# Splitting the query maxima on GpSimd instead of VectorE, and one step between them and the query features

## The chip, the cores and the metric

The kernel runs on one core of a Trainium2 chip. The metric is the device time of one execution, in microseconds: before the change the median of three runs is 328.67 us (328.09 to 328.81). The core's engines work side by side, each on its own instruction queue, in order: TensorE (PE in the profile, its weight loads PEld), VectorE (DVE), ScalarE (ACT), GpSimd (POOL) and SyncE (SP), which here only issues transfers. GpSimd's queue issues transfers too.

## The reference, cut to what matters

```
def phi(x):                                   # x: q or k, (8, 8, 576, 64)
    proj = einsum('bhsd,df->bhsf', x, w_phi)  # 128 features
    proj = proj - max(abs(proj), axis=-1)
    return concatenate([exp(proj), exp(-proj)], axis=-1)
q_p, k_p = phi(q), phi(k)
kv  = einsum('bhsf,bhsd->bhfd', k_p, v);  z = sum(k_p, axis=2)
num = einsum('bhsf,bhfd->bhsd', q_p, kv)
den = einsum('bhsf,bhf->bhs', q_p, z)[..., None] + 1e-06
x   = num / den                               # heads joined: (8, 576, 512)

h = maximum(x @ w_in, 0);  u, v = two halves of h, 512 wide each
v_n = layer norm of v;  v_s = einsum('ts,bsd->btd', w_spatial, v_n) + b_spatial
out = (u * v_s) @ w_out                       # (8, 576, 512)
```

The maximum of the absolute projections belongs to a token and a head. The change concerns the maxima of the queries alone.

## The kernel before, in words

**Stage A** (attention) works on 36 units. Each batch gives four pair units (two heads by 512 tokens), and each two batches one tail unit, which holds their last 64 tokens for all heads. In the order of the work unit 0 is a pair, unit 1 the tail of the first two batches, and later each tail unit (9, 18, 27) leads its two batches.

**Stage B** (the gated MLP of a batch) is a list of tasks that is queued when the last x of a batch has been transposed. Each step of the main loop calls `fill(0.25)` four times, which takes tasks off that list by a fixed credit, so stage B's matmuls stand between those of stage A.

Step i of the main loop (L535) writes the work of several units. Call u the unit i, w the unit i-1, z i-2, y i-3, x i-4. In this order:

- `a_keys(u)`, `a_scale(u)`: project the keys (PE L212), their maxima `mk` (DVE L224), the exponentials `kf` (ACT L227), `em` = exp of the key maxima (ACT L239), and on GpSimd v times `em`, `vs` (POOL L244 two times, L246; for a tail unit `vst`, L254 and L256)
- fill; `a_kv(z)` (PE L308, L310, then ACT L312)
- `a_queries(u)`: project the queries (PE L212) and take their maxima `mq` (DVE L233). `a_split(u)`: write them as two bf16 numbers, `mhl` = the rounded maximum (DVE L262) and what rounding left (DVE L263)
- fill; `a_transpose(i+1)` (PE L203, ACT L206 `kT`, DVE L207 `qT`); `a_max_t(w)`: transpose `mhl` of unit w on PE (L267) and copy the 16 rows to `mT` (DVE L268)
- fill; `a_x_t(x)` (PE L336, DVE L337)
- `a_qfeat(w)`: project the queries again with features on the partitions, `pq` (PE L278), subtract the maximum by a matmul of the constant `sel` with `mT` (PE L282; L287 and L289 in a tail unit), and take the exponentials `qf` (ACT L295)
- fill; `a_num(y)` (PE L327) and its division (DVE L317, L318)

So unit w's `mT` is made and used within one step, with one fill and `a_x_t` between. `mhl` and `mT` each lie in three buffers, which the units take in turn; in the listings below they are called mhl_120, mhl_124, mhl_128 and mT_122, mT_126, mT_130. The eight banks of PSUM are handed out in turn to every matmul group.

GpSimd's queue also holds the loads of q and k (L93, L94; tails L80), and stage B's layer norm: four small instructions on 128x4 or less (`root`, L381 to L384) and then `normalize` (L388), four of 128x512 for a batch.

A scheduler moves instructions a little against the order in which the code writes them, on each engine. At the start the spatial weights are loaded (`wsp`, `wspt`) and transposed after step 4 (L175, L177).

Of the kernel before, what the change touches and what calls it, by code (L numbers as in the profile page):

```python
# [9 lines left out]
BF16 = mybir.dt.bfloat16  # L10
AF = mybir.ActivationFunctionType
ALU = mybir.AluOpType
# [4 lines left out]
def kernel(  # L17
# [15 lines left out]
    nc = tc.nc  # L33

    B, H, S, D = q.shape
# [4 lines left out]
    P = 128  # L40
# [11 lines left out]
    a1 = ctx.enter_context(tc.tile_pool(name="stage_a", bufs=2))  # L52
# [93 lines left out]


    NM = 3
    mhl, mT = [], []
    for i in range(NM):  # L150
        t = cpool.tile([P, P], BF16, name=f"mhl{i}")
# [42 lines left out]
    def a_transpose(u):  # L194
        src = st[u["b"]] if u["pair"] else gs[u["g"]]
        pt = psum.tile([P, 2, 4, P], BF16, tag="bank", name="pt")
        for i, x in enumerate((src["k"], src["q"])):
            for j in range(4):
                if u["pair"]:
                    blk = x[:, 2 * u["pj"] + j // 2, (j % 2) * P:(j % 2 + 1) * P]  # L200
                else:
                    blk = x[:, 2 * j:2 * j + 2, :]
                nc.tensor.transpose(out=pt[:, i, j, :], in_=blk, identity=ident)  # L203
        u["kT"] = a1.tile([P, 4, P], BF16, tag="kT", name="kT")
        u["qT"] = a1.tile([P, 4, P], BF16, tag="qT", name="qT", bufs=3)
        nc.scalar.copy(out=u["kT"], in_=pt[:, 0])  # L206
        nc.vector.tensor_copy(out=u["qT"], in_=pt[:, 1])  # L207

# [7 lines left out]
    def a_keys(u):  # L216

        u["mk"] = small.tile([P, H], FP32, tag="mk", name="mk")
        u["kf"] = feat.tile([P, 2, H, F], BF16, tag="kf" if u["pair"] else "kf_t", name="kf",
                            bufs=4 if u["pair"] else 2)  # L220
        for half in range(2):
            pk = by_token(u["kT"], half)
            hs = slice(4 * half, 4 * half + 4)
            nc.vector.tensor_reduce(out=u["mk"][:, hs], in_=pk, axis=AX.X, op=ALU.max,  # L224
                                    apply_absolute_value=True)
            for s, sc in ((0, 1.0), (1, -1.0)):
                nc.scalar.activation(out=u["kf"][:, s, hs, :], in_=pk, func=AF.Exp, bias=0.0, scale=sc)  # L227

    def a_queries(u):
        u["mq"] = small.tile([P, H], FP32, tag="mq", name="mq")  # L230
        for half in range(2):
            pq = by_token(u["qT"], half)
            nc.vector.tensor_reduce(out=u["mq"][:, 4 * half:4 * half + 4], in_=pq, axis=AX.X, op=ALU.max,  # L233
                                    apply_absolute_value=True)

    def a_scale(u):
        em = small.tile([P, 2, H], FP32, tag="em", name="em")
        for s, sc in ((0, -1.0), (1, 1.0)):
            nc.scalar.activation(out=em[:, s, :], in_=u["mk"], func=AF.Exp, bias=0.0, scale=sc)  # L239
        if u["pair"]:  # L240
            pj = u["pj"]
            vs = feat.tile([P, 2, H, DA], BF16, tag="vs", name="vs", bufs=4)
            for s in range(2):
                nc.gpsimd.tensor_tensor(out=vs[:, s, :, 0:D], in0=st[u["b"]]["v"][:, pj * H:(pj + 1) * H, :],  # L244
                                        in1=em[:, s, :].unsqueeze(2).to_broadcast([P, H, D]), op=ALU.mult)
            nc.gpsimd.tensor_copy(out=vs[:, :, :, D:DA], in_=em.unsqueeze(3).to_broadcast([P, 2, H, 2]))  # L246
            u["vs"] = vs
        else:
            d = gs[u["g"]]
            vs = vst[u["g"] % 2]  # L250
            for bl in range(2):
                r = slice(bl * TL, (bl + 1) * TL)
                for s in range(2):
                    nc.gpsimd.tensor_tensor(out=vs[r, bl, s, :, 0:D], in0=d["v"][r],  # L254
                                            in1=em[r, s, :].unsqueeze(2).to_broadcast([TL, H, D]), op=ALU.mult)
                nc.gpsimd.tensor_copy(out=vs[r, bl, :, :, D:D + 1].rearrange("p i n o -> p i (n o)"), in_=em[r])  # L256
            d["vs"] = vs
            d["unit"] = u

    def a_split(u):  # L260
        m = mhl[u["i"] % NM]
        nc.vector.tensor_copy(out=m[:, 0:H], in_=u["mq"])  # L262
        nc.vector.tensor_tensor(out=m[:, H:2 * H], in0=u["mq"], in1=m[:, 0:H], op=ALU.subtract)  # L263

    def a_max_t(u):
        pt = psum.tile([P, P], BF16, tag="bank", name="pt")
        nc.tensor.transpose(out=pt, in_=mhl[u["i"] % NM], identity=ident)  # L267
        nc.vector.tensor_copy(out=mT[u["i"] % NM][0:2 * H, :], in_=pt[0:2 * H, :])  # L268

    def a_qfeat(u):  # L270

        m = mT[u["i"] % NM]
        u["qf"] = []
        for half in range(2):
            pq = psum.tile([P, 4, P], FP32, tag="bank", name="pq")
            if u["pair"]:
                for par in range(2):
                    nc.tensor.matmul(out=pq[:, 2 * par:2 * par + 2, :], lhsT=wphi2[:, par * F:(par + 1) * F],  # L278
                                     rhs=u["qT"][:, 2 * half:2 * half + 2, :], start=True, stop=False)
                    for x in range(2):  # L280
                        j = 4 * half + 2 * x + par
                        nc.tensor.matmul(out=pq[:, 2 * par + x, :], lhsT=sel[:, j, :], rhs=m,  # L282
                                         start=False, stop=(x == 1))
            else:
                for x in range(4):
                    h = 4 * half + x
                    nc.tensor.matmul(out=pq[:, x, :], lhsT=wphi2[:, (h % 2) * F:(h % 2 + 1) * F],  # L287
                                     rhs=u["qT"][:, h // 2, :], start=True, stop=False)
                    nc.tensor.matmul(out=pq[:, x, :], lhsT=sel[:, h, :], rhs=m, start=False, stop=True)  # L289
            if u["pair"]:  # L290
                qf = feat.tile([P, 2, 4, P], BF16, tag="qf", name="qf", bufs=7)
            else:
                qf = feat.tile([P, 2, 4, P], BF16, tag="qf_t", name="qf_t", bufs=4)
            for s, sc in ((0, 1.0), (1, -1.0)):
                nc.scalar.activation(out=qf[:, s], in_=pq, func=AF.Exp, bias=0.0, scale=sc)  # L295
            u["qf"].append(qf)
# [199 lines left out]
    def unit(i):  # L496
        return units[i] if 0 <= i < NU else None
# [30 lines left out]
    def fill(share):  # L528
        credit[0] = min(credit[0] + RATE * share, RATE / 2)
        while queue and credit[0] >= queue[0][0] / 2:  # L530
            cost, task = queue.pop(0)
            task()
            credit[0] -= cost

    def step(i):  # L535
        n, u, w, z, y, x = (unit(i + d) for d in (1, 0, -1, -2, -3, -4))
        if i == 0:
            a_transpose(u)
        if u:
            a_keys(u)  # L540
            a_scale(u)
        fill(0.25)
        if z and z["pair"]:
            a_kv(z)
        if u:
            a_queries(u)
            a_split(u)
        fill(0.25)
        if n:
            a_transpose(n)  # L550
        if w:
            a_max_t(w)
        fill(0.25)
        if x and x["pair"]:
            a_x_t(x)
            if x["pj"] == NP - 1:
                g, bl = x["g"], x["b"] % 2
                alone = g in SPLIT
                if alone or bl == 1:
                    tail_x_t(g, [bl] if alone else [0, 1])  # L560
                queue.extend(b_tasks(x["b"]))
        if w:
            a_qfeat(w)
        fill(0.25)
        if y and y["pair"]:
            a_num(y)
            if y["pj"] == NP - 1:
                g, bl = y["g"], y["b"] % 2
                alone = g in SPLIT
                if alone or bl == 1:  # L570
                    tail_num(g, [bl] if alone else [0, 1])

    def on_pair(i):
        u = unit(i)
        return u if u and u["pair"] else None

    for i in range(NU + 4):
        u = unit(i)
# [47 lines left out]
```

## Time and profile before

| what | before |
| --- | --- |
| median of three runs | 328.67 us (328.09 to 328.81) |
| the profiled execution | 327.9 us, of which span 326.1 us |
| TensorE busy | 284.8 us, 87% of the span |
| VectorE busy | 244.3 us, 75% |
| ScalarE busy | 242.3 us, 74% |
| GpSimd busy | 173.8 us, 53% |
| the two instructions of the split (L262, L263) | 36 each, 14.6 and 17.8 us of VectorE |

The span runs from the first to the last instruction; 1.8 us of the profiled execution lie around it. Times within the trace are microseconds from the start of the span. A row of a timeline gives the start, how long it lasted, the engine and line, and in brackets how long the engine had been idle ahead of it and what ended that. Rows with xN put N instructions of one line together. Matmuls overlap in PE's pipeline and their ends are modelled, so a PE that shows busy may still have short gaps in it.

### The profile page before, as it was taken

The numbers are of one execution on the slowest core, as the hardware profiler recorded it, in microseconds if no ns is written. First come the engines' busy times: TensorE is split into PE (matmuls) and PEld (weight loads), VectorE is DVE, ScalarE is ACT, GpSimd is POOL, SyncE is SP. The second block draws the span as 40 slices with busy tenths as digits, with TensorE's granted clock in tenths as the row PEclk, the third lists the DMA queues.
The fourth block names the chain that finished last, engine by engine and source line by source line (L and its number), as shares of the span: only waits on it lengthen the run. The fifth ranks groups of instructions, "written<-read, shape, count | busy, mean of one in ns | idle before, by whom it ended". The sixth has DMA issues, their size and how long they took to land.

```text
span 326.1 us, 8471 instructions
## 1 busy us (share of the span) xinstructions
PE 284.8 (87%) x3327; PEld 196.4 (60%) x3370; DVE 244.3 (75%) x626; ACT 242.3 (74%) x546; POOL 173.8 (53%) x263
## 2 busy tenths in 40 slices
PE   0485888899999899989899999999799999979884
PEld 0274677566666577657667677766577676534431
DVE  7685799698987989798798997598788983622430
ACT  3488598889498888798899668998898647433603
POOL 8299827678254756548586362527655220250520
PEclk9999899999999999999999999999999999999979
DMA  7999997931079009940732088410000004302104
GB/s 102 225 159 253 194 238 76 133 107 35 2 130 271 6 0 131 250 92 1 100 74 90 0 106 239 169 43 2 0 2 2 1 2 181 114 0 102 46 0 145
DMA packets 43773, 31.17 MB, mean 96 GB/s; under 512 B 14355, under 2 KB 38099, under 8 KB 43733
## 3 DMA queue, kind: packets, MB, share of 16 engines
q0 software_dynamic: 27856, 13.77, 31.2%
q1 hardware_dynamic: 15876, 16.85, 16.9%
q8 instruction: 26, 0.43, 0.5%
q14 instruction: 15, 0.11, 0.1%
HBM read 32.85 MB, written 9.44 MB: 130 GB/s over the span
## 4 chain that ended last, share of the span: by engine, by line
PE 39%; DVE 32%; DMA 11%; ACT 10%; POOL 4%; issue 2%; SPq 1%; POOLq 0%; ACTq 0%; DVEq 0%
PE po L468 8%; DVE mq L233 6%; PE ps L445 6%; DVE stats L374 6%; DVE mk L224 5%; DMA wspt<-in_moe_w_spatial_dram 5%; DMA out_dram<-ob 4%; PE ps L212 3%; PE pq L282 3%; ACT qf L295 3%; ACT kf L227 3%; DVE x L318 3%; PE pn L327 3%; PE pu L424 2%; PE pv L308 2%
## 5 line engine op out<-in xcount | busy, mean ns | idle before, releaser
L244 POOL TENSOR_TENSOR vs<-v_f,em 128x512 bf16<-128x512 f32 x64 | 65.5, 1044 | 56.1 <-ACT em L239 46.8
L227 ACT ACTIVATE kf<-ps 128x512 bf16<-128x512 f32 x144 | 77.4, 631 | 11.7 <-DVE mk L224 11.6
L295 ACT ACTIVATE qf<-pq 128x512 bf16<-128x512 f32 x128 | 67.1, 639 | 15.6 <-PE pq L282 15.3
L224 DVE TENSOR_REDUCE mk<-ps 128x4 f32<-128x512 f32 x72 | 47.2, 674 | 1.2 <-PE ps L212 1.1
L233 DVE TENSOR_REDUCE mq<-ps 128x4 f32<-128x512 f32 x72 | 46.4, 679 | 2.1 <-PE ps L212 2.1
L470 ACT COPY ob<-po 128x512 f32<-128x512 f32 (+1 forms) x38 | 23.2, 609 | 27.3 <-issue 17.5
L445 PE MATMUL ps<-w_spT,vn 128*128 128x512 bf16 x115 | 34.0, 392 | 5.2 <-POOL vn L388 4.5
L448 DVE TENSOR_TENSOR uT<-ps,uT 128x512 bf16<-128x512 f32 x32 | 21.9, 683 | 17.7 <-PE ps L446 17.7
L282 PE MATMUL pq<-mT,sel 128*128 128x128 bf16 x256 | 28.8, 221 | 6.8 <-DVE mT L268 6.8
L374 DVE BATCH_NORM_STATS2 stats<-vr 128x6 f32<-128x512 bf16 (+1 forms) x38 | 25.6, 681 | 12.1 <-ACT vr L373 11.8
L278 PE MATMUL pq<-qT,wphi 128*128 128x256 bf16 x128 | 31.2, 277 | 2.4 <-ACT kf L227 1.8
L424 PE MATMUL pu<-xT,w_in_bf 128*128 128x512 bf16 x120 | 31.6, 379 | 1.4 <-ACT vr L373 0.7
L371 PE MATMUL pv<-w_in_bf,xT 128*128 128x512 bf16 x118 | 31.7, 379 | 1.1 <-ACT kf L227 0.4
L468 PE MATMUL po<-w_out_bf,uT 128*128 128x512 bf16 x118 | 31.0, 379 | 0.5
L282 PEld LDWEIGHTS <-sel 128*128 128x128 bf16 x256 | 23.8, 99 | 12.5 <-issue 10.3
L206 ACT COPY kT<-pt 128x512 bf16<-128x512 bf16 x36 | 22.6, 628 | 8.4 <-PE pt L203 6.6
L373 ACT ACTIVATE vr<-pv 128x512 bf16<-128x512 f32 (+1 forms) x38 | 24.0, 639 | 6.5 <-PE pv L371 5.8
L308 PEld LDWEIGHTS <-kf 128*128 128x128 bf16 x512 | 23.7, 99 | 6.0 <-ACT qf L295 0.7
L318 DVE TENSOR_TENSOR x<-pn,rc 128x256 bf16<-128x256 f32 x64 | 26.2, 419 | 0.9
L327 PEld LDWEIGHTS <-qf 128*128 128x128 bf16 x512 | 20.5, 98 | 9.4 <-issue 4.7
L327 PE MATMUL pn<-kv,qf 128*128 128x66 bf16 x512 | 22.4, 194 | 3.6 <-ACT kv L312 2.3
L212 PE MATMUL ps<-wphi,kT 128*128 128x256 bf16 x144 | 23.3, 286 | 2.3 <-ACT kT L206 2.3
(111 smaller groups left out, 622.6 us busy)
## 6 DMA issues: line engine op xcount, KB each, us to landing
out_dram<-ob SPq DMA_DIRECT2D x32, 256.0 KB, 2.4
v_f<-in_v_dram SPq DMA_DIRECT2D x6, 1024.0 KB, 6.5
k_bf<-in_k_dram POOLq DMA_DIRECT2D x7, 512.0 KB, 6.1
q_bf<-in_q_dram POOLq DMA_DIRECT2D x7, 512.0 KB, 7.7
v_f<-in_v_dram POOLq DMA_DIRECT2D x2, 1024.0 KB, 8.7
v_tl<-in_v_dram SPq DMA_DIRECT2D x8, 128.0 KB, 4.2
w_in_bf<-in_moe_w_in_dram POOLq DMA_DIRECT2D x1, 1024.0 KB, 12.8
out_dram<-ob SPq DMA_DIRECT2D x8, 128.0 KB, 2.4
```

Source lines behind the costliest of these rows:

```text
L224: nc.vector.tensor_reduce(out=u["mk"][:, hs], in_=pk, axis=AX.X, op=ALU.max, apply_absolute_value=True)
L227: nc.scalar.activation(out=u["kf"][:, s, hs, :], in_=pk, func=AF.Exp, bias=0.0, scale=sc)
L233: nc.vector.tensor_reduce(out=u["mq"][:, 4 * half:4 * half + 4], in_=pq, axis=AX.X, op=ALU.max, apply_absolute_value=True)
L244: nc.gpsimd.tensor_tensor(out=vs[:, s, :, 0:D], in0=st[u["b"]]["v"][:, pj * H:(pj + 1) * H, :], in1=em[:, s, :].unsqueeze(2).to_broadcast( ...
L282: nc.tensor.matmul(out=pq[:, 2 * par + x, :], lhsT=sel[:, j, :], rhs=m, start=False, stop=(x == 1))
L295: nc.scalar.activation(out=qf[:, s], in_=pq, func=AF.Exp, bias=0.0, scale=sc)
L318: nc.vector.tensor_tensor(out=x, in0=pn[r, :, 0:D], in1=rc[r].to_broadcast([n, 4, D]), op=ALU.mult)
L327: nc.tensor.matmul(out=pn[:, pos, :], lhsT=u["qf"][hh][:, s, pos, :], rhs=d["kv"][:, 2 * u["pj"] + hh, s, :], start=(s == 0), stop=(s == 1))
L374: nc.vector.bn_stats(out=stats[r], in_=dst[r])
L424: nc.tensor.matmul(out=pu, lhsT=w_in_bf[:, kc, dc * P:(dc + 1) * P], rhs=d["xT"][:, kc, :], start=(kc == 0), stop=(kc == KC - 1))
L445: nc.tensor.matmul(out=ps, lhsT=d["vn"][:, sp, cs], rhs=w_spT[:, sp, 0:T0], start=(sp == 0), stop=False)
L468: nc.tensor.matmul(out=po[r], lhsT=lhs(dc), rhs=w_out_bf[:, dc, :], start=(dc == 0), stop=(dc == KC - 1))
```

## The change

The split is issued on GpSimd, other than for the first seven units (0 to 6), which keep it on VectorE. `a_qfeat` is called for unit z instead of w, that is one step later than `a_max_t` of the same unit. `qT`, which then lives a step longer, gets five buffers instead of three. The unused function `on_pair` goes.

```diff
+    EARLY = 7
...
-        u["qT"] = a1.tile([P, 4, P], BF16, tag="qT", name="qT", bufs=3)
+        u["qT"] = a1.tile([P, 4, P], BF16, tag="qT", name="qT", bufs=5)
...
     def a_split(u):
         m = mhl[u["i"] % NM]
-        nc.vector.tensor_copy(out=m[:, 0:H], in_=u["mq"])
-        nc.vector.tensor_tensor(out=m[:, H:2 * H], in0=u["mq"], in1=m[:, 0:H], op=ALU.subtract)
+        eng = nc.vector if u["i"] < EARLY else nc.gpsimd
+        eng.tensor_copy(out=m[:, 0:H], in_=u["mq"])
+        eng.tensor_tensor(out=m[:, H:2 * H], in0=u["mq"], in1=m[:, 0:H], op=ALU.subtract)
...
-        if w:
-            a_qfeat(w)
+        if z:
+            a_qfeat(z)
         fill(0.25)
```

Three places show what this does to the queues. In the changed kernel the line numbers are one higher up to the split and two higher behind it.

VectorE, where unit 8 is split (buffer mhl_128) and unit 7's transposed maxima are copied (mT_126). Before:

```order
L233 TENSOR_REDUCE mq<-ps 128x4 x2
L207 COPY qT<-pt 128x512
L262 CAST mhl_128<-mq 128x8
L268 COPY mT_126<-pt 16x128
L263 TENSOR_TENSOR mhl_128<-mq,mhl_128 128x8
L337 COPY xT<-pt 128x512
```

and now:

```order
L234 TENSOR_REDUCE mq<-ps 128x4 x2
L208 COPY qT<-pt 128x512
L270 COPY mT_126<-pt 16x128
L339 COPY xT<-pt 128x512
L367 COPY xTt<-pt 128x4x64
```

The two instructions of the split are gone from VectorE's queue, here and for every unit from 7 on, 58 in all.

GpSimd at the same stage, from the tail unit 9 (its last instruction is the CAST to vst_138) to unit 10, with the layer norm of the first batch between. Before:

```order
L256 CAST vst_138<-em 64x16
L381 TENSOR_SCALAR var<-mv 128x4
L382 TENSOR_TENSOR rs<-var,neghalf 128x4
L383 TENSOR_TENSOR var<-mv,rs 128x4
L384 TENSOR_SCALAR rs<-var 128x4
L388 TENSOR_SCALAR vn<-vr,rs 128x512 x4
L244 TENSOR_TENSOR vs<-v_f,em 128x8x64 x2
L246 CAST vs<-em 128x16x2
```

and now:

```order
L257 CAST vst_138<-em 64x16
L264 CAST mhl_120<-mq 128x8
L265 TENSOR_TENSOR mhl_120<-mq,mhl_120 128x8
L383 TENSOR_SCALAR var<-mv 128x4
L384 TENSOR_TENSOR rs<-var,neghalf 128x4
L385 TENSOR_TENSOR var<-mv,rs 128x4
L386 TENSOR_SCALAR rs<-var 128x4
L390 TENSOR_SCALAR vn<-vr,rs 128x512 x4
L245 TENSOR_TENSOR vs<-v_f,em 128x8x64 x2
L247 CAST vs<-em 128x16x2
L264 CAST mhl_124<-mq 128x8
L265 TENSOR_TENSOR mhl_124<-mq,mhl_124 128x8
```

The split stands behind the unit's product with v, and behind whatever layer norm was queued ahead of that. The transfers that GpSimd issues keep their order; they now have the split between them.

TensorE at the first places where the query features follow the transpose of the maxima with nothing between, the transpose being that of buffer mhl_124 (unit 1). Before:

```order
L267 LDWEIGHTS mhl_124
L267 MATMUL pt<-ident,mhl_124 128x128
L287 LDWEIGHTS wphi_76
L287 MATMUL pq<-qT,wphi_76 128x128
L287 LDWEIGHTS wphi_76
L287 MATMUL pq<-qT,wphi_76 128x128
L289 LDWEIGHTS sel
L289 MATMUL pq<-mT_126,sel 128x128
```

and now:

```order
L269 LDWEIGHTS mhl_124
L269 MATMUL pt<-ident,mhl_124 128x128
L280 LDWEIGHTS wphi_76
L280 MATMUL pq<-qT,wphi_76 128x256
L284 LDWEIGHTS sel
L284 MATMUL pq<-mT_122,sel 128x128
```

The matmuls with `sel` read the `mT` of the unit before (mT_122, unit 0) instead of the one whose transpose has just been issued (mT_126, unit 1). At the start this also means that the features of unit 2, not those of unit 3, are the last ahead of the transposes of the spatial weights. At the end the features of the last two units stand one step later among stage B's last matmuls of batch 6.

More of the change, by code (lines that the diff above doesn't have):

```diff
@@ L571, in step @@
                     tail_num(g, [bl] if alone else [0, 1])
-    def on_pair(i):
-        u = unit(i)
-        return u if u and u["pair"] else None
     for i in range(NU + 4):
```

## The prediction

> **What bounds the kernel now.** I read the page's busy line and chain first, then a table of stages, then PE's waits in the long middle stage.
>
> ```profile
> PE 284.8 (87%) x3327; PEld 196.4 (60%) x3370; DVE 244.3 (75%) x626; ACT 242.3 (74%) x546; POOL 173.8 (53%) x263
> PE 39%; DVE 32%; DMA 11%; ACT 10%; POOL 4%; issue 2%; SPq 1%; POOLq 0%; ACTq 0%; DVEq 0%
> ```
>
> PE is busiest and holds most of the chain of waits, but DVE holds a third of it. No engine bounds the whole, so the stage matters. The split of units 7 to 35, which moves, lies between 52 and 270 us:
>
> ```profile
> core 0: us, PE busy (x) PEld busy (x) DVE busy (x) ACT busy (x) POOL busy (x), PEclk, DMA share, GB/s
> 52.00:270.00 218.00, 204.60 (x2581) 147.04 (x2616) 185.12 (x472) 183.41 (x424) 123.73 (x184) 1.00 0.39 76
> 270.00:326.00 56.00, 47.06 (x349) 23.20 (x353) 19.89 (x50) 23.45 (x42) 13.53 (x26) 0.96 0.25 85
> ```
>
> There PE works 94% of the time, DVE 85%, ACT 84%. PE is in order and stands still 218.00 - 204.60 = 13.4 us. Whatever takes those stops away shortens the stage. The waits of PE between 52 and 270 us say what they are (line, releaser, us in total, times, longest):
>
> ```profile
> PE pq L282 <- DVE mT L268: 6.3, 11, 1.2
> PE pq L278 <- ACT kf L227: 1.6, 3, 0.7
> PE pq L289 <- DVE mT L268: 1.4, 2, 1.1
> ...
> PE pn L327 <- DVE mq L233: 0.3, 1, 0.3
> ```
>
> 6.3 + 1.4 = 7.7 us, more than half, is one wait: the matmul with `sel` waits for DVE's copy of the transposed maxima. One such place, around the tail unit 18:
>
> ```profile
> 143.06 0.22 PE L267 MATMUL pt<-ident,mhl 128*128 128x128 bf16 x1
> ...
> 144.56 2.04 POOL L244 TENSOR_TENSOR vs<-v_f,em 128x512 bf16<-128x512 f32 x2 [4.42 <-issue]
> ...
> 145.65 0.98 DVE L262 CAST mhl<-mq 128x8 bf16<-128x8 f32 x1
> ...
> 147.04 0.18 DVE L268 COPY mT<-pt 16x128 bf16<-16x128 bf16 x1
> ...
> 147.27 0.22 PE L289 MATMUL pq<-mT,sel 128*128 128x128 bf16 x1 [1.13 <-DVE mT L268]
> ```
>
> The transpose ended at 143.28, but its copy came at 147.04, behind DVE's queue, with the next unit's split in it. The cast of 8 numbers per partition took 0.98 us there and ended at 146.63, just as GpSimd's two products did (144.56 + 2.04 = 146.60). The split's cost on DVE is mostly such waiting:
>
> ```profile
> L262 DVE CAST mhl<-mq x36: 157/334/1128, 15.0 to 262.5; 128x8 bf16<-128x8 f32 x36
> L263 DVE TENSOR_TENSOR mhl<-mq,mhl x36: 122/481/1085, 15.2 to 262.9; 128x8 bf16<-128x8 f32 x36
> 52.00:270.00 218.00, 12.62 (x29) 1.00 0.39 76
> 52.00:270.00 218.00, 15.01 (x29) 1.00 0.39 76
> ```
>
> The last two rows are these lines' busy time in the stage: 12.62 + 15.01 = 27.6 us for 29 units, 0.95 us each, against 157 + 122 ns for the shortest of the two.
>
> **The change part by part.**
>
> *The features one step later.* A unit's `mT` is now copied in one step and first read in the next. A step lasts about 7.5 us (218 us for 29), longer than the 3.8 us from transpose to copy above, so the 7.7 us of stops go. Bounds: 7.7 us if PE meets nothing else late, and nothing if each is replaced. The next things late on PE are in the list above, ACT's `kf` and DVE's `mq`: small, and not tied to this order. I take 7.0 us. The 8.7 - 7.7 = 1.0 us of such waits before 52 us I don't count, since a transfer ends that stage (below).
>
> ```profile
>   DVE mT L268: 8.7, 15
> ```
>
> *27.6 us off DVE.* Nothing is queued on DVE in their place. What that brings beyond the stops is bounded below by nothing (DVE is off the end of the stage) and above by the split's share of the chain of waits, which was largest between 60 and 110 us:
>
> ```profile
> by line: DMA out_dram<-ob 13.4%; DVE mq L233 9.5%; DVE stats L374 8.8%; DVE mk L224 8.5%; ACT qf L295 8.3%; DVE x L318 5.7%; ACT kf L227 5.6%; DVE mhl L262 4.7%; ACT vr L373 4.1%; DVE uT L448 3.8%; DVE mhl L263 3.4%; PE pq L282 3.2%; DVE qT
> ```
>
> There it is 4.7 + 3.4 = 8.1% of 50 us. PE has only 13.4 - 7.7 = 5.7 us of other visible stops to give, so that is the upper end here. I take 0.7 us, near the lower end: those stops name ACT more than DVE.
>
> *58 small instructions on GpSimd.* The trace has no split there. Nearest rows by shape:
>
> ```profile
> L382 POOL TENSOR_TENSOR rs<-var,neghalf 128x4 f32<-128x4 f32 x8 | 8.3, 1043 | 0.7
> L246 POOL CAST vs<-em 128x32 bf16<-128x32 f32 x32 | 6.8, 212 | 6.3 <-ACT em L239 6.3
> L383 POOL TENSOR_TENSOR var<-mv,rs 128x4 f32<-128x4 f32 x8 | 1.6, 205 | 0.6
> ```
>
> and the distance from one dependent instruction to the next:
>
> ```profile
> 223.05 0.20 POOL L383 TENSOR_TENSOR var<-mv,rs 128x4 f32<-128x4 f32 x1
> 223.34 0.25 POOL L384 TENSOR_SCALAR rs<-var 128x4 f32<-128x4 f32 x1
> ```
>
> A cast of 128x32 is 0.21 us, a product of 128x4 0.21 us, start to start 0.29: about 0.6 us a unit, 17 us in all; GpSimd goes to 124 + 17 = 141 of 218 us. From above, both like L382, a power: 2 x 1.04 + 0.2 = 2.3 us a unit. From below, DVE's 0.28. The split is a cast and a plain subtraction, so I take 0.6.
>
> What waits for GpSimd is new: PE's `a_max_t` (L267), and the whole of PE behind it. Queued behind the split on GpSimd are the next `vs`, the layer norm and the loads. The split stands behind the unit's `vs`, so its slack is from the end of L246 to L267 of the same unit. The pairs of units 7, 10, 29 and 30:
>
> ```profile
> 56.45 0.21 POOL L246 CAST vs<-em 128x32 bf16<-128x32 f32 x1
> 57.86 0.22 PE L267 MATMUL pt<-ident,mhl 128*128 128x128 bf16 x1
> ...
> 80.19 0.21 POOL L246 CAST vs<-em 128x32 bf16<-128x32 f32 x1
> 81.44 0.22 PE L267 MATMUL pt<-ident,mhl 128*128 128x128 bf16 x1
> ...
> 217.92 0.21 POOL L246 CAST vs<-em 128x32 bf16<-128x32 f32 x1
> 222.89 0.22 PE L267 MATMUL pt<-ident,mhl 128*128 128x128 bf16 x1
> ...
> 228.74 0.21 POOL L246 CAST vs<-em 128x32 bf16<-128x32 f32 x1
> 230.04 0.22 PE L267 MATMUL pt<-ident,mhl 128*128 128x128 bf16 x1
> ```
>
> They leave 1.2, 1.0, 4.8 and 1.1 us. Five of the 29 units leave under 1.4 us, the first and the last of them being 7 and 30 and their sum 6.0; the others, like 29, leave over 2. With 0.6 us a unit only unit 10 is late: unit 9's split stands in the same unbroken run of GpSimd, so 80.40 + 1.2 = 81.6, late by 0.2. Steps that shorten by some 0.2 us take that from every slack. I take a loss of 0.5 us, between 0 and 5.5 (at 2.3 us a unit the five lose 11.5 - 6.0).
>
> The Trainium skill speaks against the move: GPSIMD Engine Reference, section 4.1 Engine selection, wants elementwise work on VectorE and calls GpSimd about twice as slow for two inputs. Applied to DVE's means here (435 and 518 ns) an estimate by that page is 0.44 + 1.04 = 1.5 us a unit; the five narrow units would lose 7.5 - 6.0 = 1.5 us instead of 0.5, and the sum below would be 323.2. Applied to DVE's shortest it is 0.4 us a unit, which the rows above bear out better.
>
> *The start.* Until 38 us all goes at the pace of a transfer:
>
> ```profile
> 38.12 0.22 PE L177 MATMUL pt<-ident,wspt 64*128 64x64 bf16 x1 [1.06 <-DMA wspt<-in_moe_w_spatial_dram]
> ...
> 39.00 2.06 ACT L295 ACTIVATE qf<-pq 128x512 bf16<-128x512 f32 x4 [1.33 <-PE pq L282]
> ...
> 39.93 0.61 PE L212 MATMUL ps<-wphi,kT 128*128 128x256 bf16 x4
> ...
> 41.48 0.60 ACT L227 ACTIVATE kf<-ps 128x512 bf16<-128x512 f32 x1
> ```
>
> Units 0 to 6 stay on DVE, and that load is issued ahead of any split on GpSimd, so it lands as before. Unit 3's features, which ACT made from 39.00 on, now come a step later, so ACT has nothing until the keys of 39.93 are through: at most 40.5 - 39.0 = 1.5 us of ACT's time lost, at least nothing. I take 0.7.
>
> *The end.* The features of two units move into a stretch where PE is filled with stage B's last tasks; PE has the same sum to do. Cover gone, it would cost the four exponentials of a unit, 2.06 us. I take 0. `qT`'s buffers cost nothing: no transfer and no instruction more.
>
> Sum: -7.0 - 0.7 + 0.5 + 0.7 = -6.5 us. The profiled execution took 327.9 us (326.1 of span and 1.8 around it), so 321.4. The runs' median lies 328.67 - 327.9 = 0.8 above that execution: **322.2 us**.
>
> **The rivals.**
>
> *More than the stops.* If DVE's split paced the stage together with PE, its removal also closes other stops. Most it can give is all of PE's 13.4 us; I price it at 10 to 13: 316 to 319. For it: 8.1% of the chain in one stretch. Against: ACT, at 183.4 of 218 us, is not relieved.
>
> *Another wait takes its place.* PE arrives 0.27 us a step earlier at matmuls that need ACT's `kT` and `kf` or a bank of PSUM, and stands there instead. Then the 7.7 us come back but for a little: 327.5 to 329.3. For it: ACT's 84%. Against: 13 of PE's stops named `mT` and few named ACT.
>
> *GpSimd is late for PE (slower).* One mechanism: PE's L267 waits for the split behind `vs` and the layer norm. It decides against the change when two instructions on GpSimd cost some 2.3 us a unit. The five narrow units then lose 5.5 us, GpSimd goes to 124 + 67 = 191 of 218 us, and its `vs` and layer norm fall behind by 0.5 us in about ten more units: -6.5 - 0.5 + 5.5 + 5 = +3.5, 332.2 us (330 to 335). For it: 1.04 us on L382. Against: L246 and L383.
>
> *The change does not do what it says.* Excluded by the two queues: the split has left DVE's, and L284 reads the earlier `mT`.
>
> **How the numbers follow.** Forecast 0.61 (own range 319.5 to 325.5: the taken value, and its terms moved half way to their bounds), more than the stops 0.14, another wait 0.13, GpSimd late 0.12. Low 317.0 leaves out the far half of the second, high 328.2 the upper part of the third and all of the last. A measurement of this kernel tells 0.2% (0.66 us) from no change, which is 328.0 to 329.3. The third case lies there for 0.09 of its 0.13 and below for 0.04. So faster 0.61 + 0.14 + 0.04 = 0.79, same 0.09, slower 0.12.
>
> **What would show it.** Right, if PE's waits name `mT` for under 1 us, the stage of units 7 to 35 is 6 to 7 us shorter, and the split on GpSimd shows 0.2 to 0.3 us for each instruction. PE waiting for `mhl` on GpSimd for over 2 us would show the term of 0.5 too small; PE waits on ACT grown by 5 us the third case; a DVE gap with no PE stop left, the second. I am wrong if the stage keeps its length although the waits for `mT` are gone.

## The result and the profile after

| what | before | after | forecast |
| --- | --- | --- | --- |
| median, runs side by side on one chip | 328.38 us (327.0 to 328.81) | 319.53 us (318.53 to 319.81) | 322.2 us (317.0 to 328.2) |
| ratio | | 0.973, 95% interval 0.970 to 0.977 | 0.980 |
| the profiled execution, its span | 327.9, 326.1 us | 318.53, 316.8 us | 321.4 us |

Medians and ranges here and below leave out executions that took over 1.5% longer than the fastest of their kernel.

The change makes the kernel faster by 2.7%, by 8.9 us from median to median. In the same unit as the forecast's sum, the profiled execution, it brought 327.9 - 318.5 = 9.4 us where the sum had 6.5. Both profiled executions were faster than their medians, the one before by 0.5 us and the one after by 1.0.

The busy line and the engines' part in the chain of waits, after:

```profile
PE 284.4 (90%) x3370; PEld 196.6 (62%) x3370; DVE 223.7 (71%) x568; ACT 241.0 (76%) x546; POOL 183.5 (58%) x321
PE 66%; DVE 10%; DMA 7%; ACT 7%; POOL 6%; issue 1%; SPq 1%; POOLq 0%; ACTq 0%; DVEq 0%
```

DVE's share of the chain fell from 32% to 10%, and PE, with the same matmuls to do, now holds two thirds of it. Note the matmul count: all 3370 were recorded here, 3327 in the profile of before. So a little of what the trace of before showed as idle PE was PE at work.

To see where the time went, both spans are cut at the same two places of the program: the transposes of the query maxima (`a_max_t`) of units 7 and 35. The stretches are the start, the 28 steps in between, and the end. First before, then after (columns: length, busy time and count of PE, PEld, DVE, ACT, POOL, PE's granted clock, DMA share, GB/s):

```profile
0.00:57.86 57.86, 38.01 (x489) 30.45 (x490) 44.60 (x123) 41.32 (x96) 40.63 (x58) 0.97 1.11 178
57.86:267.44 209.58, 197.22 (x2471) 140.97 (x2505) 178.58 (x452) 176.28 (x407) 119.68 (x179) 1.00 0.38 77
267.44:326.10 58.66, 49.57 (x376) 25.01 (x379) 21.13 (x53) 24.75 (x44) 13.53 (x26) 0.96 0.24 82
```

```profile
0.00:57.02 57.02, 36.59 (x478) 29.81 (x478) 46.20 (x121) 38.78 (x91) 41.09 (x60) 0.94 1.13 180
57.02:256.68 199.66, 196.04 (x2506) 140.76 (x2505) 156.42 (x395) 175.54 (x407) 128.87 (x235) 1.00 0.40 81
256.68:316.80 60.12, 51.74 (x395) 26.00 (x391) 21.12 (x53) 26.71 (x48) 13.56 (x26) 0.96 0.24 80
```

The middle stretch became 209.58 - 199.66 = 9.9 us shorter. Two more profiles of the unaltered changed kernel show it 200.3 and 199.7 us long, so it varies by some 0.6 us. The start became 0.8 us shorter and the end 1.5 us longer, but one unit's features went from the first to the last (PE's 12 weight loads for it: 490 to 478, and 379 to 391; about 1 us of PE's time, by the timeline of another unit, 139.68 to 140.73), so neither place lost or won as much as 1 us beside that. The end varies more than that from profile to profile, and with the clock granted in it: with the same features in it, it took 58.4 us at a clock of 0.99, 59.6 to 60.1 at 0.96 and 61.4 to 61.6 at 0.93. In the middle PE stood idle for 199.66 - 196.04 = 3.6 us, before for 12.4 by the trace. Of these 12.4 an estimated 1.5 to 2 are the 35 matmuls missing there: a second profile of the changed kernel that lacks 37 of them (below) shows 5.7 us idle. So PE's visible stops went from some 10.5 us to 3.6.

What is left of them in the middle stretch of the changed kernel, and the one wait for `mT` in its whole span, which lies in the start (line, releaser, us, times, longest):

```profile
PE pq L280 <- ACT kf L228: 1.9, 2, 1.1
PE pv L373 <- DVE xTt L367: 0.4, 1, 0.4
...
PE ps L447 <- POOL vn L390: 0.3, 1, 0.3
```

```profile
PE pv L310 <- DVE mT L270: 0.6, 1, 0.6
```

No wait for `mT` is left in the middle, and no matmul waits for `mhl`. The same place that the prediction showed, the tail unit 18, now reads:

```profile
138.36 0.22 PE L269 MATMUL pt<-ident,mhl 128*128 128x128 bf16 x1
...
141.37 0.18 DVE L270 COPY mT<-pt 16x128 bf16<-16x128 bf16 x1
...
145.31 0.22 PE L291 MATMUL pq<-mT,sel 128*128 128x128 bf16 x1
```

The copy still comes 2.8 us after the transpose, behind DVE's queue. But nobody needs it before 145.31.

The split itself, by its lines (shortest, median, longest in ns; first and last start), and from the same view how long PE's weight loads sat idle until it was there (us, times):

```profile
L264 POOL CAST mhl<-mq x29: 181/191/205, 56.5 to 253.2; 128x8 bf16<-128x8 f32 x29
L265 POOL TENSOR_TENSOR mhl<-mq,mhl x29: 195/201/217, 56.8 to 253.4; 128x8 bf16<-128x8 f32 x29
L264 DVE CAST mhl<-mq x7: 157/306/1033, 14.6 to 47.9; 128x8 bf16<-128x8 f32 x7
L265 DVE TENSOR_TENSOR mhl<-mq,mhl x7: 135/168/1001, 14.8 to 49.0; 128x8 bf16<-128x8 f32 x7
...
  POOL mhl L265: 0.2, 1
```

On GpSimd it takes 0.19 + 0.20 = 0.39 us, every time. In the seven units that DVE kept, it still reaches 1.0 us for one instruction.

### The profile page after: what moved, and what is told of

The parts are those of the page before. It is cut to its first block, busy times and chain, and to the rows that moved or that the text cites. A ratio compares the mean times of both kernels' runs of the same rounds, so it can differ in the third digit from the quotient of the medians.

```text
span 316.8 us, 8543 instructions
## 1 busy us (share of the span) xinstructions
PE 284.4 (90%) x3370; PEld 196.6 (62%) x3370; DVE 223.7 (71%) x568; ACT 241.0 (76%) x546; POOL 183.5 (58%) x321
## 4 chain that ended last, share of the span: by engine, by line
PE 66%; DVE 10%; DMA 7%; ACT 7%; POOL 6%; issue 1%; SPq 1%; POOLq 0%; ACTq 0%; DVEq 0%
PE po L470 11%; PE ps L447 9%; PE ps L213 8%; PE pv L373 6%; PE pu L426 5%; DMA wspt<-in_moe_w_spatial_dram 5%; PE pv L310 4%; PE pn L329 4%; PE pt L204 4%; PE pq L280 3%; PE pq L284 3%; DVE stats L376 3%; ACT kf L228 3%; POOL vn L390 3%; PE ps L448 2%; DMA bsp_row<-in_moe_b_spatial_dram 2%
## 5 line engine op out<-in xcount | busy, mean ns | idle before, releaser
L447 PE MATMUL ps<-w_spT,vn 128*128 128x512 bf16 x128 | 35.4, 392 | 4.4 <-POOL vn L390 4.4
L280 PE MATMUL pq<-qT,wphi 128*128 128x256 bf16 x128 | 30.3, 274 | 3.2 <-ACT kf L228 2.1
L284 PE MATMUL pq<-mT,sel 128*128 128x128 bf16 x256 | 30.3, 220 | 0.0
L284 PEld LDWEIGHTS <-sel 128*128 128x128 bf16 x256 | 25.1, 98 | 5.7 <-issue 3.6
L208 DVE COPY qT<-pt 128x512 bf16<-128x512 bf16 x36 | 15.1, 420 | 17.2 <-ACT kT L207 17.2
```

The lines of the kernel that those rows point to most:

```text
L447: nc.tensor.matmul(out=ps, lhsT=d["vn"][:, sp, cs], rhs=w_spT[:, sp, 0:T0], start=(sp == 0), stop=False)
```

## The experiments

Two theories stood at the outset. A, the forecast's: the later step takes away PE's stops for `mT`, and that is nearly all; DVE's relief brings little. B: the relief of DVE carries a good part of the gain itself, since DVE's queue is what makes `mT` and other things late.

### The step alone

```diff
-    EARLY = 7
+    EARLY = 99
```

The split of all units stays on DVE; the features come a step later.

> The features one step later, the split left on VectorE for all units. Theory A (the gain is TensorE's stops for the copied maxima): these stops go with the step alone, 7.0 of the stage's us, so 321 to 322.5 us, with under 1 us of TensorE waits that name mT. Theory B (VectorE's 27.6 us of splits pace the stage): VectorE keeps them all, so little comes, 325.5 to 328 us.

Measured: 322.74 us (320.36 to 324.75), ratio to the kernel before 0.982 (0.975 to 0.990). The middle stretch, and PE's waits in it that are over 0.4 us:

```profile
57.45:260.59 203.14, 198.01 (x2507) 141.09 (x2505) 178.91 (x451) 175.38 (x407) 119.34 (x179) 1.00 0.40 79
```

```profile
PE pq L280 <- ACT kf L228: 2.0, 2, 1.2
PE pv L373 <- DVE xTt L367: 0.8, 2, 0.6
```

203.14 against 209.58: the step brings 6.4 us there, and no wait for `mT` is left. DVE works as long as before (178.9 us). The rest of the change, 203.14 - 199.66 = 3.5 us, is then the split's. Theory B's 325.5 to 328 is excluded, and theory A's mechanism is borne out, though the time lies 0.2 us above its range. From median to median of the runs beside it (327.57 us before) the step brought 4.8 us.

### The split alone

```diff
-        if z:
-            a_qfeat(z)
+        if w:
+            a_qfeat(w)
```

The split is on GpSimd from unit 7 on; the features stay in the step of `a_max_t`.

> The split on GpSimd from unit 7 on, the features in the same step as the transpose of the maxima, as before. Theory A: the copy of the maxima stands less deep in VectorE's queue, since 0.95 us a unit is gone from it, but is still read in the same step; about half of the 7.7 us of stops goes, 324 to 326 us, and 3 to 5 us of TensorE waits still name mT. Theory B: nearly all of the gain, 319.5 to 322 us.

Measured: 322.35 us (321.27 to 323.67), ratio 0.982 (0.976 to 0.988). The middle stretch, and the largest of PE's waits in it:

```profile
56.89:260.25 203.36, 197.93 (x2507) 140.88 (x2505) 157.11 (x396) 176.06 (x407) 128.53 (x235) 1.00 0.40 79
```

```profile
PE pq L284 <- DVE mT L270: 2.2, 5, 0.8
```

This is where theory A fails. Without the later step the split's move brings 6.2 us in the middle, almost as much as the step. It does so by the same stops: with the split out of DVE's queue `mT` is copied sooner, and PE's waits for it shrink to 2.2 + 0.2 us (the second at L291). So the two parts are cures for the same stops, and by the waits they overlap: the step alone takes away all 7.7 us, the split's move alone 5.3. In the middle stretch they bring 6.4 and 6.2 us alone and 9.9 together, from one profile of each. The medians can't tell this: 4.8 and 5.2 us alone make 10.0, where both together bring 8.9, and the runs of one kernel spread over more than that difference. Theory B's range (319.5 to 322) is 0.4 us away, within the spread of the runs.

Both kernels have `qT`'s five buffers, so neither shows what these bring by themselves. Before the change DVE's copy into `qT` waited this much, and for nothing else (us, times):

```profile
  ACT kT L206: 10.1, 13
```

It never waited for PE to be done with an old `qT`, so there was no such stop for more buffers to take away.

### All units on GpSimd

```diff
-    EARLY = 7
+    EARLY = 0
```

> The changed kernel with the split on GpSimd for all units, the first seven too. If the first seven stand on VectorE to keep GpSimd's queue free for the transfers of the start: the splits of units 0 and 1 and their waits stand ahead of or between these, wspt lands 0.6 to 2 us later than 38.1, and as much comes on the time, 320 to 321.5 us. Rival: the splits fit between the issues and the landing stays at 38, 319 to 319.8 us.

Measured: 323.16 us (322.27 to 324.57), ratio 0.984 (0.978 to 0.991): the changed kernel loses some 3 us by it, more than the 320 to 321.5 expected. The transpose of unit 7 came at 61.14, not 57.02. PE's waits until there that are not for a transfer, and GpSimd's queue:

```profile
PE pv L312 <- POOL vst L257: 5.0, 1, 5.0
PE pt L269 <- POOL mhl L265: 4.2, 2, 2.7
...
PE pt L269 <- ACT kT L207: 2.5, 1, 2.5
```

```profile
22.36 0.80 POOL L136 DMA_DIRECT2D w_out_bf<-in_moe_w_out_dram  x1
23.16 2.07 POOL L255 TENSOR_TENSOR vst<-v_tl,em 64x512 bf16<-64x512 f32 x2
...
27.80 0.19 POOL L264 CAST mhl<-mq 128x8 bf16<-128x8 f32 x1
...
28.95 0.20 POOL L265 TENSOR_TENSOR mhl<-mq,mhl 128x8 bf16<-128x8 f32 x1
```

In the first 30 us GpSimd issues the transfers of the weights, and unit 1's products stand behind these issues, and its split behind those: it ends at 29.15. Nothing here is late because of the split's own 0.4 us. Nor is it the reason that was expected: the load of `wspt` was issued at 21.83, no later than in the changed kernel (22.3), and PE did not wait for it. So the units that kept the split on DVE did so with cause, but not all seven: with `EARLY = 4`

```diff
-    EARLY = 7
+    EARLY = 4
```

> The changed kernel with the split on GpSimd from the 5th unit on, not the 8th (the first four on VectorE). A try for a faster kernel. Theory (the first units on GpSimd stand behind the issue of transfers there, and cost 4 us at the start when all are): those that are left come after the issues, so the start is within 1 us of the changed kernel's, 319 to 321. Rival (each unit of the first seven on GpSimd costs its share of the 4 us): +1.5 us, 321.5.

it took 319.49 us (318.19 to 320.23), beside 318.68 us (317.93 to 319.94) of the changed kernel on the same chip: nothing won, and nothing lost that these runs can show.

### The last unit's features moved back

```diff
-        if z:
-            a_qfeat(z)
+        if z and i <= NU:
+            a_qfeat(z)
+        if i == NU:
+            a_qfeat(w)
```

> The changed kernel with the features of the last unit moved back to the step of the unit before, so that the end stands as before the change. The prediction's term for the end is 0: 319.5 us within 0.7. Rival: the later features hold up the end by the four exponentials of a unit or part of them, then 317.5 to 318.8 us.

Measured: 320.69 us (318.71 to 321.65), ratio 0.975 (0.967 to 0.983). That is above the 319.5 within 0.7 that was expected, and away from the rival's 317.5 to 318.8. The end took 61.37 us at a clock of 0.93, beside 61.52 at the same clock in the kernel with `EARLY = 4`, whose end is that of the changed kernel. No gain: that the last features come later at the end costs nothing that can be measured.

### VectorE's time put back, without the split

What did the split's move bring beyond the stops for `mT`: DVE's time, or something about the split? Here the changed kernel gets work on DVE that nobody reads, at the split's old place. In the first kernel:

```diff
+        if u["i"] >= EARLY:
+            dum = small.tile([P, 2, 6], FP32, tag="dum", name="dum")
+            x = u["qT"].rearrange("p a b -> p (a b)")
+            nc.vector.bn_stats(out=dum[:, 0, :], in_=x[:, 0:128])
```

> The changed kernel, and for each unit from the 7th on VectorE takes the statistics of 128 columns of qT once more, with nothing reading the result: some 0.28 us a unit (an estimate from the shortest records of the two split instructions on VectorE, 0.148 + 0.122 us), 8 us in all, put back on VectorE in the place of the split, but in a form that has no part in GpSimd's work. Theory (time on VectorE is paid in short gaps of PE, at about the rate of 3.5 us for the 27.6 us that the split alone took off it): +0.3 to +1.5 us over the changed kernel, 319.8 to 321. Rival (what costs is VectorE waiting for GpSimd, not its time): within 0.5 us of the changed kernel.

and in the second a larger one ahead of it:

```diff
+            nc.vector.bn_stats(out=dum[:, 0, :], in_=x[:, 0:512])
+            nc.vector.bn_stats(out=dum[:, 1, :], in_=x[:, 0:128])
```

> The same with the statistics of 512 and of 128 columns: some 0.95 us a unit, 27 us in all, about what the split's means cost on VectorE before. Theory (VectorE's time is what is paid): +3 to +4 us over the changed kernel, 322.5 to 323.5, the same as with the features moved and the split left on VectorE (322.7); VectorE's busy time in the stage of units 7 to 35 again near 183 us, PE's busy time there near 198 us. Rival (the place of the split in the chain, or the waiting for GpSimd, is what is paid): at most +1.5 us, below 321.

The changed kernel, once more beside them:

> The changed kernel once more, unaltered, beside the three others on the same chip: 318.5 to 320 us. It is what they are compared with.

Measured: 319.98 us (319.24 to 320.91) for the changed kernel, 320.28 (319.37 to 321.87) with 0.28 us a unit, 323.35 (321.97 to 324.63) with 0.96. The middle stretch of the three, in this order:

```profile
57.29:257.59 200.30, 194.57 (x2469) 140.84 (x2505) 156.44 (x395) 175.54 (x407) 128.87 (x235) 1.00 0.40 80
```

```profile
57.05:258.43 201.38, 194.98 (x2470) 140.90 (x2505) 161.32 (x423) 175.44 (x407) 128.91 (x235) 1.00 0.40 80
```

```profile
57.07:261.84 204.77, 196.31 (x2471) 141.41 (x2505) 176.72 (x452) 176.28 (x407) 128.97 (x235) 0.99 0.39 79
```

The dummies themselves, and the largest of PE's waits with them, in the kernel with 0.96 us:

```profile
L267 DVE BATCH_NORM_STATS2 dum<-qT x29: 664/683/696, 53.4 to 251.8; 128x6 f32<-128x512 bf16 x29
L268 DVE BATCH_NORM_STATS2 dum<-qT x29: 259/276/285, 54.0 to 252.5; 128x6 f32<-128x128 bf16 x29
```

```profile
PE pv L378 <- DVE xTt L372: 2.8, 2, 1.7
```

The records of the dummies add up to 27 us there, but DVE is busy for only 20.3 us more, since the records of neighbouring instructions on DVE overlap. With these 20.3 us the middle stretch is 4.5 us longer, and the median 3.4 us higher: about as much as the step alone lacked. So DVE's time is what is paid, at about a fifth of its length, and neither the split's place in the chain from maxima to features nor its contention with GpSimd is needed for it. PE pays in two ways: in visible waits for DVE's later copies (2.8 us for `xTt`), and in gaps too short to be listed. The second is a reading of the busy times: with equal numbers of matmuls recorded PE was busy for 198.01 us with the step alone and for 196.04 after, 2.0 of the 3.5 us. With the smaller dummy the middle stretch is 1.1 us longer for 4.9 us more on DVE, which fits this rate, but the median is only 0.3 us higher and the runs overlap those of the changed kernel: it decides nothing between theory and rival.

### A dearer split on GpSimd

The prediction's rival on the slow side said that GpSimd would be late for PE from some 2.3 us a unit on. Here the split reads a copy of the maxima that GpSimd makes first, spread to 512 columns (two copies in a row), or one copy of 512, or one of 256 columns (below, the kernel with two copies; the others have `range(1)`, and for 256 columns 32 in place of 64):

```diff
+        src = u["mq"]
+        if u["i"] >= EARLY:
+            for k in range(2):
+                dum = a1.tile([P, 64, H], FP32, tag=f"dum{k}", name=f"dum{k}", bufs=1)
+                nc.gpsimd.tensor_scalar(out=dum, in0=src.unsqueeze(1).to_broadcast([P, 64, H]) if k == 0 else src,
+                                        scalar1=1.0, scalar2=None, op0=ALU.mult)
+                src = dum
+            src = src[:, 0, :]
-        eng.tensor_copy(out=m[:, 0:H], in_=u["mq"])
-        eng.tensor_tensor(out=m[:, H:2 * H], in0=u["mq"], in1=m[:, 0:H], op=ALU.subtract)
+        eng.tensor_copy(out=m[:, 0:H], in_=src)
+        eng.tensor_tensor(out=m[:, H:2 * H], in0=src, in1=m[:, 0:H], op=ALU.subtract)
```

> The changed kernel, and for each unit from the 7th on GpSimd takes two copies of 128x512 floats in a row ahead of the split, which reads the second: the split then comes some 1.6 us or more later (an estimate, no such copy is in the trace), 2.0 to 2.2 us from its start with its own 0.4 us, about the point from which the prediction's rival of a late GpSimd decides. Theory (the step between split and features leaves that much slack): less than +2 us, below 321.5, PE waiting for mhl less than 1 us in all. Rival (GpSimd is late for PE as soon as its two instructions cost 2.2 us): +5 to +10 us, 325 to 330, with PE waiting for mhl 4 us or more.

> The same with one copy of 128x512 floats, 1.49 us: copy and split make some 1.9 us a unit. Theory (cover): six to eight of 29 units are late, by 1.5 us less their cover, 4 to 6 us of waits for mhl, and what GpSimd then does later besides; +4 to +10 us, 323.5 to 330, well under half of the 42 us that two copies cost. The prediction's rival of a late GpSimd put the point at 2.3 us a unit and the price of all units late at 10 us: between the two, near 325. Rival (in proportion): +21 us, 341.

> As with two copies ahead of the split on GpSimd, but one copy of 128x256 floats: 0.75 us (half of the 1.49 us that a copy of 128x512 took there), so that the two instructions and the copy make some 1.15 us a unit. Theory (the split on GpSimd has a cover that is used up bit by bit: in the changed kernel it ends 0.06 us to 5.6 us ahead of PE's use, the median 3.05 us, three of 29 units under 0.75 us): PE waits 1 to 2 us for mhl in all, +1 to +3 us over the changed kernel, 320.5 to 322.5. Rival (it is GpSimd's use as such that costs, from the first tenth on): 42 us for 2.99 us a unit makes 10.5 us at this rate, 330.

The latter two ran with the kernel with `EARLY = 4` and with the changed kernel once more on one chip:

> The changed kernel once more, unaltered, beside these three on the same chip: 318.5 to 320.5 us.

| on GpSimd for a unit | median | over the changed kernel beside it |
| --- | --- | --- |
| split alone, 0.39 us | 318.68 us (317.93 to 319.94) | |
| with 256 columns, 0.39 + 0.86 = 1.25 us | 324.56 us (323.6 to 325.83) | +5.9 |
| with 512 columns, 0.39 + 1.50 = 1.89 us | 329.43 us (328.37 to 331.03) | +10.8 |
| with twice 512 columns, 0.39 + 2.99 = 3.38 us | 361.88 us (358.94 to 363.56) | +41.9 (to 319.98) |

The copies in the kernels with 256 and with 512 columns, by their line:

```profile
L268 POOL TENSOR_SCALAR dum<-mq x29: 848/855/897, 58.1 to 258.9; 128x256 f32<-128x256 f32 x29
```

```profile
L268 POOL TENSOR_SCALAR dum<-mq x29: 1487/1496/1537, 57.2 to 265.2; 128x512 f32<-128x512 f32 x29
```

The middle stretch of the three, from 256 columns up:

```profile
59.58:262.36 202.78, 197.46 (x2505) 140.88 (x2506) 155.83 (x393) 174.92 (x406) 153.38 (x263) 1.00 0.39 78
```

```profile
59.33:268.71 209.38, 198.66 (x2504) 141.81 (x2505) 155.81 (x392) 174.82 (x405) 171.06 (x263) 0.99 0.37 75
```

```profile
62.64:302.09 239.45, 204.88 (x2467) 146.51 (x2505) 156.35 (x391) 174.88 (x400) 212.54 (x291) 0.96 0.32 65
```

PE's waits for the split in each, in the matmul and in the weight load ahead of it (two records of one wait, not to be added):

```profile
PE pt L277 <- POOL mhl L273: 4.1, 4, 2.0
PEld L277 <- POOL mhl L273: 5.3, 6, 2.2
```

```profile
PE pt L277 <- POOL mhl L273: 8.6, 5, 3.3
PEld L277 <- POOL mhl L273: 12.0, 8, 3.4
```

```profile
PE pt L277 <- POOL mhl L273: 32.1, 13, 4.7
PEld L277 <- POOL mhl L273: 34.9, 15, 4.9
```

DVE's and ACT's busy times are those of the changed kernel (156.4 and 175.5), so GpSimd's extra work slowed neither: most of what is paid is PE waiting for `mhl`. For 256 columns the waits, 4 to 5 us, are below the 5.9 of the medians. By the profiles 3.1 us lie in the middle stretch, 2.6 ahead of it (0.9 of them PE's wait for unit 7's split), and 1.5 in the end, at a clock of 0.93 against 0.96, so some 4 us can be put down to the split. The price is neither nothing up to a point nor proportional, but rises: by the medians about 6 us for the first 0.86 us a unit, 5 for the next 0.64, 31 for the last 1.49. At the last GpSimd is busy for 212.54 of 239.45 us, issues of transfers not counted, and sets the pace beside PE. Its part in the chain of waits there, where it had 6% in the changed kernel:

```profile
PE 37%; POOL 32%; DMA 9%; DVE 8%; ACT 6%; issue 5%; SPq 1%; POOLq 0%; ACTq 0%; DVEq 0%
```

The expectations missed: with two copies both the theory (below 321.5) and its rival (325 to 330) were far too low, and for 256 columns 1 to 3 us was. That last one took each unit's distance from the end of its split to PE's use, one by one. For units 7 and 10 it was right: both splits end 0.06 us ahead of PE in the changed kernel, and with 256 columns PE waits 0.93 and 0.97 us for them. Nearly half of the 4.1 us is unit 20. Its split, in the changed kernel first and with 256 columns second:

```profile
147.59 0.19 POOL L264 CAST mhl<-mq 128x8 bf16<-128x8 f32 x1
147.86 0.20 POOL L265 TENSOR_TENSOR mhl<-mq,mhl 128x8 bf16<-128x8 f32 x1
148.02 2.04 POOL L245 TENSOR_TENSOR vs<-v_f,em 128x512 bf16<-128x512 f32 x2
```

```profile
153.13 0.85 POOL L268 TENSOR_SCALAR dum<-mq 128x256 f32<-128x256 f32 x1
153.96 2.03 POOL L245 TENSOR_TENSOR vs<-v_f,em 128x512 bf16<-128x512 f32 x2
...
156.36 0.20 POOL L273 TENSOR_TENSOR mhl<-dum,mhl 128x8 bf16<-128x8 f32 x1
```

```profile
156.61 0.23 PE L277 MATMUL pt<-ident,mhl 128*128 128x128 bf16 x1 [1.98 <-POOL mhl L273]
```

In the changed kernel this split ends 1.81 us ahead of PE, more than the copy costs. But here the scheduler put the unit's product with v between the copy and the split, 2.2 us that stood behind it before. The same happens in the kernel with 512 columns, where PE waits 3.27 us for unit 20, so these kernels differ from the changed one in the order of GpSimd's queue too, and not all of their price is the length of the copy. What is left of the 4.1 us is delay that was handed on: GpSimd has no idle stretch from 156.8 to 178.1 us with 256 columns, and unit 23, whose split ends 1.91 us ahead in the changed kernel, makes PE wait 0.21.

## Why the prediction was right, and where not

**The step later: 7.0 taken, 6.4 measured.** The step alone shortened the middle stretch by 6.4 us and left no wait for `mT` in it. The mechanism is shown, and the size was near; by the medians, whose runs spread by some 4 us, it was 4.8.

**27.6 us off DVE: 0.7 taken, 3.5 measured.** This is the term that was mis-sized, and the reason why 9.4 us came and not 6.5. It was set near the lower end of its bounds (0 to 5.7) because PE's other visible stops named ACT more than DVE. Two things were overlooked. The stops that are listed aren't all that PE loses to DVE: by the busy times some 2.0 us of the 3.5 lie in gaps that no list shows. And DVE's share of the chain, 32% before, 25% with the step alone and 10% after, told that DVE mattered, which the releasers of the remaining stops did not. The 27.6 us themselves add up records that overlap their neighbours: DVE's busy time in the middle stretch fell by 22. The upper end of 5.7 held, although it was taken from 13.4 us of idle PE, in which the missing matmul records stood too.

**The two parts as terms of one sum.** The sum treated the move off DVE as what comes on top of the step. That was the right way to add them, since in the middle stretch alone each brings over 6 us and together 9.9. But the text didn't see that the split's move by itself takes away most of the same stops: of 7.7 us of waits for `mT`, 2.4 are left in the middle with it alone. Theory A, which drew on the same view, expected 324 to 326 us of that run, and it took 322.35.

**The split on GpSimd: a loss of 0.5 taken, 0.2 seen.** 0.6 us a unit was forecast and 0.39 came. Unit 10, named as the one that would be late, was the one that PE's weight load waited for, 0.2 us. The estimate by the Trainium skill (GPSIMD Engine Reference, section 4.1 Engine selection) from DVE's means, 1.5 us a unit, is not borne out; the one from DVE's shortest, 0.4, is.

**The start and the end: 0.7 and 0 taken, about 0 each measured,** once the moved features are counted. ACT's lost time at the start did not show. With the last unit's features moved back the kernel is not faster.

**The rivals.** *More than the stops* had its mechanism half right: DVE did pace the stage beside PE, as the dummies on it show. But it had all of the visible stops closed, and 3.6 us of them are left. The time, 319.53, lies between it (316 to 319) and the forecast of 322.2, and nearer to it. *Another wait takes its place* did not happen: PE's waits for ACT's `kf` are 2.2 us in the middle, where they were 1.6 us between 52 and 270. *GpSimd is late for PE* was the right thing to be afraid of, and its price was set too far out. At 1.9 us a unit, not at 2.3, the kernel is no faster than before (ratio 1.003, 0.999 to 1.007), and 1.25 us already cost 4 to 6 us. By the prediction's working, with five narrow units and 6.0 us of slack among them, 1.25 us a unit would have cost some 0.3 us (5 x 1.25 - 6.0). Three things went past that working. The slack shrank by more than the 0.2 us taken: unit 7, with 1.2 us before, had 0.06 left after 0.4 us of split. The order of GpSimd's queue changed at unit 20. And a delay was handed on beyond units 9 and 10. A split of 1.5 us a unit, the estimate named above, would by the table have taken between 5.9 and 10.8 us and not 1.5; this too is an estimate, for a queue whose order changes as with these copies.

What stays open: how much of the dearer split's price is its length and how much the changed order; and how PE's gaps within its busy time come about one by one, since the ends of matmuls are modelled and no list shows them.

## What to carry to other kernels

A small instruction on the busiest in-order helper engine costs more than its wait shows: put time back on that engine, in a form that nobody reads, and see what the whole kernel pays (here about a fifth of it). Two cures for the same stop need not add, so try each alone before a sum is made of them. Before work goes to another engine, ask for that engine's room as a queue and not unit by unit, and look at the order of that queue afterwards: 0.4 us a unit cost next to nothing on GpSimd here, 1.25 us cost 4 to 6 us, and 1.9 us the whole gain.

## What the runs showed of the hardware

A cast or subtraction of 128x8 on GpSimd took 0.18 to 0.22 us in all 58 cases. On DVE the same two took 0.12 us at best and 1.13 us at worst before the change; the ones that took over 0.5 us ended within 0.1 us of the end of an instruction on GpSimd, as in the prediction's place at tail unit 18 (146.63 and 146.60). The statistics of 128x512 that were put on DVE at the same place took 0.66 to 0.70 us in all 29 cases, 11 of which began while a product on GpSimd was running: that form was never held up. The Trainium skill (SBUF — State Buffer, section Who interferes with whom) describes this: DVE and GpSimd share a pair of ports, casts in some modes and instructions with two inputs in SBUF (for reading) need it, whoever comes second is blocked until the first is through, and an instruction outside those modes with one input is not. The durations agree with it. The same skill (Perfetto Trace Analysis, section Optimizing Scalar/DVE Operations) warns that moving work between these two might therefore not help. Here it did, by 6.2 us of the middle stretch alone.

A copy with a factor from floats to floats took GpSimd 0.86 us for 256 columns and 1.50 us for 512: 2.5 ns a column and 0.2 us besides (1.50 - 0.86 = 0.64 us for 256). The layer norm's line on 512 columns of bf16, the same operation with two factors, takes 0.76 us (3.04 us for four at 74.78 in the changed kernel).
